# Moving value loads and reordering the first units in a fused attention and SwiGLU kernel

## The chip, the cores and the metric

The kernel runs on one core of a Trainium2 chip. The metric is the device time of one execution in microseconds. A profile, taken by the hardware profiler, covers the span from the first to the last instruction, which is a little shorter than the device time. The engines are TensorE (PE in the profile; its weight loads are PEld), VectorE (DVE), ScalarE (ACT), GpSimd (POOL) and SyncE (SP).

## The reference

The reference is attention with a sliding window and a few sink positions, followed by a SwiGLU feed-forward block. The batch is 4, there are 8 heads of 64, the sequence is 768, the window is 128 and there are 4 sinks.

```python
scores = scale * np.matmul(q, k.transpose(0, 1, 3, 2))
keep = is_sink | in_window          # pos < 4, or 0 <= row - pos < 128
scores = np.where(keep, scores, -1000000000.0)
scores = scores - np.max(scores, axis=-1, keepdims=True)
a = np.exp(scores)
a = a / (np.sum(a, axis=-1, keepdims=True) + 1e-09)
attn = np.matmul(a, v)
# x: 3072 tokens x 512, the heads side by side
g = x @ w_gate                      # 512 x 1536
silu = g * (1.0 / (1.0 + np.exp(-g)))
val = x @ w_val                     # 512 x 1536
out = silu * val @ w_out            # 1536 x 512
```

All inputs and the output are float32; the kernel computes its matrix products in bfloat16.

## The kernel before

The tokens are worked on in 12 groups of 256 (three for each batch entry). For a group, `step_T` or `step_TN` transposes keys and queries, `step_S` makes scores and exponentials, `step_PV` multiplies with the values and normalises, and `step_X` transposes the result for the projections. Group 0 has an opening of its own (`pair_T`, `pair_S`, `pair_mask`), which the change leaves alone. The projections are made in units: `gate` makes 512 columns of the gate projection (`gate_a`), takes the attention steps that the schedule hangs on that unit, and makes the value projection and the product (`gate_b`). Blocks 0 and 1 are the tokens of groups 0 and 1, at 256 tokens each; "01" means both together. A unit at f of block 0 covers f and f + 1, and each weight pair `load_gate(i)` holds two values of f, so that units f = 0, 2, 4 of a block need weight pairs 0, 1, 2.

[...] `later` is a list of VectorE work put off until `flush`. All loads on `nc.gpsimd` go out from GpSimd in program order and convert float32 to bfloat16 on the way. [...]

```python
    def load_rows(g):
        b, c = divmod(g, GC)
        x = new_rows(g)
        for i in range(2):
            for w in range(2):
                nc.gpsimd.dma_start(
                    x[64 * w:64 * (w + 1), i],
                    by_rows((k, q)[i], b, w, ALL, c * 256))


    ...

    def load_v(g):
        b, c = divmod(g, GC)
        va = vpool.tile([P, 2, H, VS], BF16, tag=f"va{g}", name="va")
        nc.vector.memset(va[:, :, :, D:D + 1], 1.0)
        for j in range(2):
            t0 = c * 256 + j * P
            nc.gpsimd.dma_start(
                va[:, j, :, 0:D], v[b, :, t0:t0 + P].rearrange("h p d -> p h d"))
        vas[g] = va

    ...

    load_sinks(vcf, 0, 1)
    for i in range(2):
        nc.gpsimd.dma_start(x0[:, i, 4:8], by_two((k, q)[i], 4))
    nc.gpsimd.iota(tq, [[1, P]], base=0, channel_multiplier=0,
                   allow_small_or_imprecise_dtypes=True)
    nc.gpsimd.iota(tk, [[0, 1]], base=0, channel_multiplier=1,
                   allow_small_or_imprecise_dtypes=True)
    load_rows(1)
    load_v(0)
    nc.gpsimd.iota(th8, [[-32, 4], [-NS, 4]], base=0, channel_multiplier=1,
                   allow_small_or_imprecise_dtypes=True)
    load_gate(0)
    load_gate(1, (0,))
    load_v(1)
    load_gate(1, (1,))
    load_gate(2)
    nc.gpsimd.tensor_copy(out=vcf[64:128], in_=vcf[0:64])

    ...

    def step_T(g, i, p2, evict=None):
        b, c = divmod(g, GC)
        new_T(b)
        x = rows[g]
        pt = bank([P, 2, 256], FP32, "pt")
        for pp in range(2):
            p = 2 * p2 + pp
            for r in range(4):
                for w in range(2):
                    h = slice(64 * w, 64 * (w + 1))
                    nc.tensor.matmul(
                        pt[h, pp, r:256:4], x[h, i, p, r * D:(r + 1) * D],
                        ident[h, h], start=True, stop=True, skip_group_check=True)
        dst = (kTs, qTs)[i][b][:, 2 * p2:2 * p2 + 2, c * 256:(c + 1) * 256]
        if (evict or ("a", "v")[i]) == "a":
            nc.scalar.copy(out=dst, in_=pt)
        else:
            nc.vector.tensor_copy(out=dst, in_=pt)

    ...

    def step_S(g, p2):          # scores of four heads, exp on ScalarE, mask on VectorE later
        ...
        pss = [bank([P, 512], FP32, "s") for _ in range(4)]
        for pp in range(2):
            p = 2 * p2 + pp
            for kk, qq, n, col in parts:
                for h in range(2):
                    r = slice(h * D, (h + 1) * D)
                    nc.tensor.matmul(
                        pss[2 * pp + h][:, col:col + n], kTs[b][r, p, kk:kk + P],
                        qTs[b][r, p, qq:qq + n], start=True, stop=True)
        ...
        for pp in range(2):
            h0 = 4 * p2 + 2 * pp
            for h in range(2):
                nc.scalar.activation(
                    e_t[g][:, h0 + h, lo:512], pss[2 * pp + h][:, lo:512],
                    AF.Exp, scale=scale)

            def dve(e=e_t[g][:, h0:h0 + 2, lo:512]):
                nc.vector.tensor_tensor(
                    e, e, m[:, :, lo:512].broadcast_to([P, 2, 512 - lo]), op=ALU.mult)
            later.append(dve)


    ...

    def step_PV(g, j, hh, norm="v"):   # P@V of four heads of one 128-row half
        ...
        xn = xns[g, j][:, 256 * hh:256 * (hh + 1)].rearrange("p (h d) -> p h d", h=4)

        def dve():
            rcp = smallp.tile([P, 4, 1], FP32, tag="rcp", name="rcp")
            nc.vector.reciprocal(rcp, po[:, :, D:D + 1])
            if norm == "a":
                for hq in range(4):
                    nc.scalar.activation(
                        xn[:, hq], po[:, hq, 0:D], AF.Copy, scale=rcp[:, hq])
            else:
                nc.vector.tensor_tensor(
                    xn, po[:, :, 0:D], rcp.broadcast_to([P, 4, D]), op=ALU.mult)
        if norm == "a":
            dve()
        else:
            later.append(dve)


    ...

    def project(ws, tb, f, name):
        n = xTs[tb].shape[2]
        ps = bank([P, 512], FP32, name)
        for i in range(512 // n):
            fi, fo = FOF[f + i]
            for c in range(DMC):
                nc.tensor.matmul(
                    ps[:, i * n:(i + 1) * n], ws[fi][:, c, fo * P:(fo + 1) * P],
                    xTs[tb][:, c], start=(c == 0), stop=(c == DMC - 1))
        return ps

    def gate_a(tb, f):
        if tb not in hts:
            n = SIZES[tb]
            t = hpool.tile([P, DFC * 512], BF16, tag="ht", name="ht")
            hts[tb] = dense(t, DFC, n)
            if tb == 0:
                hts["01"] = t.rearrange("p (b c n) -> p b c n", b=2, c=DFC)
                hts[1] = t[:, DFC * n:2 * DFC * n].rearrange("p (c n) -> p c n", c=DFC)
        pg = project(wgs, tb, f, "pg")
        th = tpool.tile([P, 512], FP32, tag="th", name="th")
        nc.scalar.activation(th, pg, AF.Tanh, scale=0.5)
        return pg, th

    def gate_b(tb, f, pg, th):
        pv = project(wvs, tb, f, "pv")
        u = upool.tile([P, 512], BF16, tag="u", name="u")
        nc.vector.scalar_tensor_tensor(u, th, 1.0, pg, op0=ALU.add, op1=ALU.mult)
        if tb == "01":
            nc.vector.tensor_tensor(
                hts[tb][:, :, f], *(x.rearrange("p (b n) -> p b n", b=2) for x in (u, pv)),
                op=ALU.mult)
            return
        nc.vector.tensor_tensor(
            hts[tb][:, f:f + 512 // SIZES[tb]].rearrange("p a n -> p (a n)"), u, pv,
            op=ALU.mult)

    def gate(tb, f, attn):
        a = gate_a(tb, f)
        for step in attn:
            step()
        gate_b(tb, f, *a)
        flush()

    def both(one_, two_, attn):

        a = [gate_a(*x) for x in (one_, two_)]
        for x, y in zip((one_, two_), a):
            gate_b(*x, *y)
        flush()

    ...

    def pro(*steps):
        for s in steps:
            s()
            if len(later) > 1:
                later.pop(0)()

    ...

    pair_S(3, 2)
    for p in range(1, NP2):
        pair_mask(p)
    nc.vector.tensor_scalar(lt8, th8, float(NS), None, op0=ALU.is_lt)
    nc.vector.scalar_tensor_tensor(lt8, th8, 0.0, lt8, op0=ALU.is_ge, op1=ALU.mult)
    nc.vector.tensor_reduce(diag_h, lt8.rearrange("p q h -> p h q"), mybir.AxisListType.X,
                            op=ALU.max)
    step_vsb(0)
    load_nat(2)
    load_gate(3)
    load_v(2)
    load_gate(4)
    load_gate(5)
    for i in range(4):
        load_out(i)
    step_T(1, 0, 0, "a")
    step_T(1, 0, 1, "a")
    step_T(1, 1, 0, "a")
    step_PV(0, 0, 0)
    step_PV(0, 0, 1)
    flush()
    step_T(1, 1, 1, "a")
    step_ks(0)
    step_PV(0, 1, 0)
    step_PV(0, 1, 1)
    flush()
    step_S(1, 0)
    masks1 = list(later)
    later.clear()
    step_X(0, 0)
    step_X(0, 1)
    flush()
    step_S(1, 1)
    later[:0] = masks1
    flush()
    load_nat(3)
    load_v(3)
    nc.gpsimd.memset(vcl, 0.0)
    nc.gpsimd.memset(vcl[:, :, D:D + 1], 1.0)
    load_sinks(vcl, 1, B)

    g0, g1, g2 = gates(0), gates(1), gates(2)
    us = [g0[0], g0[1], (alone, 0, 0), (both, g0[2][1:], g1[0][1:]), g1[1],
          g1[2], *((gate, "01", f) for f in range(6, DFC)),
          *g2, *downs(0), *downs(1), *downs(2)]

    ...

    weave(us, slots(
        (0, [K(1)]), (1, [A(step_PV, 1, 0, 0), A(step_PV, 1, 0, 1, "a"), A(step_PV, 1, 1, 0),
                              A(step_PV, 1, 1, 1, "a"), flush]),
        (2, [A(step_X, 1, 0, "a"), A(step_X, 1, 1, "now")]),
        ((4, 4, 5, 5), TN(2)), ((6, 7), Ss(2)), (6, [K(2)]),
        ...
```

The whole kernel follows.

Of the kernel before, what the change touches and what calls it, by code (L numbers as in the profile page):

```python
# [14 lines left out]
def kernel(  # L15
# [12 lines left out]
    nc = tc.nc  # L28
# [66 lines left out]
    def load_rows(g):  # L95
        b, c = divmod(g, GC)
        x = new_rows(g)
        for i in range(2):
            for w in range(2):
                nc.gpsimd.dma_start(  # L100
                    x[64 * w:64 * (w + 1), i],
                    by_rows((k, q)[i], b, w, ALL, c * 256))
# [90 lines left out]
    load_rows(1)  # L193
    load_v(0)
    nc.gpsimd.iota(th8, [[-32, 4], [-NS, 4]], base=0, channel_multiplier=1,
                   allow_small_or_imprecise_dtypes=True)
    load_gate(0)
    load_gate(1, (0,))
    load_v(1)
    load_gate(1, (1,))  # L200
# [9 lines left out]
    def flush():  # L210
        for f in later:
            f()
        later.clear()
# [208 lines left out]
    def gate_a(tb, f):  # L422
        if tb not in hts:
            n = SIZES[tb]
            t = hpool.tile([P, DFC * 512], BF16, tag="ht", name="ht")
            hts[tb] = dense(t, DFC, n)
            if tb == 0:
                hts["01"] = t.rearrange("p (b c n) -> p b c n", b=2, c=DFC)
                hts[1] = t[:, DFC * n:2 * DFC * n].rearrange("p (c n) -> p c n", c=DFC)
        pg = project(wgs, tb, f, "pg")  # L430
        th = tpool.tile([P, 512], FP32, tag="th", name="th")
        nc.scalar.activation(th, pg, AF.Tanh, scale=0.5)  # L432
        return pg, th

    def gate_b(tb, f, pg, th):
        pv = project(wvs, tb, f, "pv")
# [18 lines left out]
    def both(one_, two_, attn):  # L455

        a = [gate_a(*x) for x in (one_, two_)]
        for x, y in zip((one_, two_), a):
            gate_b(*x, *y)
        flush()  # L460
# [139 lines left out]
    for p in range(1, NP2):  # L600
        pair_mask(p)
    nc.vector.tensor_scalar(lt8, th8, float(NS), None, op0=ALU.is_lt)
# [9 lines left out]
    for i in range(4):  # L612
        load_out(i)
    step_T(1, 0, 0, "a")
    step_T(1, 0, 1, "a")
    step_T(1, 1, 0, "a")
    step_PV(0, 0, 0)
    step_PV(0, 0, 1)
    flush()
    step_T(1, 1, 1, "a")  # L620
    step_ks(0)
    step_PV(0, 1, 0)
    step_PV(0, 1, 1)
    flush()
    step_S(1, 0)
    masks1 = list(later)
    later.clear()
    step_X(0, 0)
    step_X(0, 1)
    flush()  # L630
    step_S(1, 1)
    later[:0] = masks1
    flush()
# [7 lines left out]
    us = [g0[0], g0[1], (alone, 0, 0), (both, g0[2][1:], g1[0][1:]), g1[1],  # L641
          g1[2], *((gate, "01", f) for f in range(6, DFC)),
# [8 lines left out]
    def NV(g):  # L651
# [3 lines left out]
        (0, [K(1)]), (1, [A(step_PV, 1, 0, 0), A(step_PV, 1, 0, 1, "a"), A(step_PV, 1, 1, 0),  # L655
                              A(step_PV, 1, 1, 1, "a"), flush]),
        (2, [A(step_X, 1, 0, "a"), A(step_X, 1, 1, "now")]),
        ((4, 4, 5, 5), TN(2)), ((6, 7), Ss(2)), (6, [K(2)]),
        ((8, 8), PVs(2)[:2]), (9, [A(step_PV, 2, 0, 1, "a"), A(step_PV, 2, 1, 1, "a")]),
        ((10, 11), [A(step_X, 2, 0, "a"), A(step_X, 2, 1, "a")]),  # L660
        (11, [NV(4), lambda: nc.gpsimd.tensor_copy(out=vcl[64:128], in_=vcl[0:64])]), ((14, 14, 15, 15), TN(3, "aa")),
        (15, [A(xbar, 4)]), (15, [NV(5)]), (19, [A(xbar, 5)]), (19, [NV(6)]),
        (23, [A(xbar, 6)]), (23, [NV(7)]),
        ((17, 18), Ss(3)), (18, [A(step_ks, 1)]), (18, [A(step_vsb, 1)]),
        ((19, 19, 19, 20), PVs(3)), (20, Xs(3)),
        ((19, 20), Ss(4)), (19, [K(4)]),
        ((21, 21, 22, 22), PVs(4)), (22, Xs(4))))
# [56 lines left out]
```

## Time and profile before

| what | value |
|---|---|
| median of 3 runs | 238.88 us (238.76 to 239.7) |
| span of the profiled execution | 237.3 us |
| mean granted TensorE clock | 0.998 |
| PE idle, span from 0 to 30 us | 2.79 us (27.21 busy of 30.00) |
| moved over the span | 27.36 MB, mean 115 GB/s |

The page gives for each engine its busy time and share of the span, and digits for 40 equal slices of the span, of about 5.9 us each. The change touches the first five or six slices. Four rows of digits show the opening against the rest (tenths of busy time for the engines; for DMA the mean busy share of the 16 DMA engines):

```profile
DVE  4888778768652888960798980688970598877000
ACT  4896485467452836512845622655622663333221
POOL 8996865720807107080260700080000000000000
DMA  8999999994999999999499994599204100200132
```

In the groups of the page, "u<-th,pg" is the first of two VectorE products of a unit (tanh plus one, times the gate projection), "ht<-u,pv" the second. "e<-s" is the exponential of scores, "e<-e,mask" the mask, "xn<-o,rcp" the normalisation of P@V, "px" and "xT" the transposed result. A timeline row gives start, duration, engine, line, operation, tiles and count, and in brackets the idle time before it with what ended it.

### The profile page before, as it was taken

The page shows a single profiled execution, that of the slowest core. Times are in us where ns is not written, and L with a number is a line of the kernel's source. Part 1 is how long each engine was busy: PE and PEld are TensorE (multiplying, and loading weights), DVE is VectorE, ACT ScalarE, POOL GpSimd, SP SyncE. Part 2 cuts the span into 40 slices and gives each one's busy share as a digit, 9 for nine tenths or more (in the row PEclk, how much of TensorE's full clock was granted, in tenths as well). Part 3 has the DMA queues.
Part 4 walks back from the last instruction along what each step waited for, and adds up shares of the span by engine and source line. Part 5 has one row for each costly group of instructions (what it writes and reads, how often), then busy time and mean ns, then how long its engine had stood idle before and what let it go on. Part 6 is the DMA issues. An engine that isn't in the chain of part 4 may idle for free.

```text
span 237.3 us, 4886 instructions
## 1 busy us (share of the span) xinstructions
PE 229.4 (97%) x1874; PEld 127.3 (54%) x1901; DVE 157.9 (67%) x335; ACT 114.5 (48%) x237; POOL 74.5 (31%) x98
## 2 busy tenths in 40 slices
PE   7899999999999999999999999999999999999994
PEld 4577845795554444444444444444444445488443
DVE  4888778768652888960798980688970598877000
ACT  4896485467452836512845622655622663333221
POOL 8996865720807107080260700080000000000000
PEclk9999999999999999999999999999999999999999
DMA  8999999994999999999499994599204100200132
GB/s 140 152 179 178 180 200 205 159 148 74 132 138 202 155 130 107 138 118 239 112 123 114 116 73 145 138 96 137 40 21 139 64 3 0 44 3 1 52 127 89
DMA packets 107655, 27.36 MB, mean 115 GB/s; under 512 B 94704, under 2 KB 104688, under 8 KB 107632
## 3 DMA queue, kind: packets, MB, share of 16 engines
q0 software_dynamic: 76640, 13.90, 79.0%
q1 hardware_dynamic: 30448, 12.89, 27.6%
q8 instruction: 15, 0.25, 0.4%
q10 hardware_dynamic: 544, 0.26, 0.4%
q14 instruction: 8, 0.07, 0.1%
HBM read 28.34 MB, written 6.29 MB: 146 GB/s over the span
## 4 chain that ended last, share of the span: by engine, by line
PE 88%; ACT 5%; DVE 2%; issue 1%; DMA 1%; SPq 0%; DVEq 0%; ACTq 0%
PE pd L475 26%; PE pv L417 26%; PE pg L417 25%; PE o L355 4%; PE s L292 4%; ACT e L299 2%; DMA st<-in_k_dram 1%; ACT e L572 1%; PE pn L245 1%; ACT xn L366 1%; PE o L335 1%; PE pk L320 1%; ACT th L432 1%; DVE u L438 1%; PE px L396 0%
## 5 line engine op out<-in xcount | busy, mean ns | idle before, releaser
L438 DVE SCALAR_TENSOR_TENSOR u<-th,pg 128x512 bf16<-128x512 f32 x72 | 49.1, 682 | 39.2 <-ACT th L432 39.2
L417 PE MATMUL pv<-xT,wv 128*128 128x512 bf16 (+1 forms) x351 | 73.0, 336 | 0.9 <-DMA wv<-in_moe_w_val_dram 0.4
L417 PE MATMUL pg<-xT,wg 128*128 128x512 bf16 (+1 forms) x351 | 73.1, 335 | 0.7
L432 ACT ACTIVATE th<-pg 128x512 f32<-128x512 f32 x72 | 43.5, 604 | 62.4 <-PE pg L417 58.7
L475 PE MATMUL pd<-wo,ht 128*128 128x512 bf16 (+2 forms) x291 | 64.8, 370 | 0.4
L444 DVE TENSOR_TENSOR ht<-u,pv 128x512 bf16<-128x512 bf16 x66 | 45.4, 688 | 10.4 <-PE pv L417 3.5
L417 PEld LDWEIGHTS <-wg 128*128 128x128 bf16 x360 | 35.0, 98 | 28.2 <-issue 0.9
L299 ACT ACTIVATE e<-s 128x512 bf16<-128x512 f32 (+1 forms) x88 | 42.7, 583 | 3.5 <-PE s L292 3.5
L475 PEld LDWEIGHTS <-ht 128*128 128x128 bf16 x300 | 27.9, 98 | 29.9 <-issue 0.5
L417 PEld LDWEIGHTS <-wv 128*128 128x128 bf16 x360 | 32.0, 98 | 21.1 <-issue 1.7
L111 POOL DMA_DIRECT2D nat<-in_k_dram x20 | 17.6, 887 | 75.9 <-DMA qT<-nat 72.9
L480 ACT ACTIVATE ot<-pd 128x512 f32<-128x512 f32 (+1 forms) x24 | 14.3, 596 | 47.4 <-PE pd L475 43.4
L304 DVE TENSOR_TENSOR e<-e,mask 128x1024 bf16<-128x1024 bf16 (+1 forms) x44 | 27.2, 651 | 4.2 <-ACT e L299 4.2
L122 POOL DMA_DIRECT2D va<-in_v_dram x24 | 21.5, 920 | 4.3 <-DMA wo<-in_moe_w_out_dram 2.5
L369 DVE TENSOR_TENSOR xn<-o,rcp 128x256 bf16<-128x256 f32 x44 | 18.7, 424 | 1.5
L355 PEld LDWEIGHTS <-e 128*128 128x128 bf16 x352 | 15.0, 98 | 7.8 <-DVE va L119 0.2
L111 POOL DMA_DIRECT2D nat<-in_q_dram x20 | 17.7, 896 | 1.4 <-DMA wg<-in_moe_w_gate_dram 0.8
L355 PE MATMUL o<-va,e 128*128 128x65 bf16 x352 | 17.0, 193 | 0.2
L292 PE MATMUL s<-qT,kT 64*128 64x128 bf16 (+1 forms) x240 | 12.9, 237 | 0.0
L292 PEld LDWEIGHTS <-kT 64*128 64x128 bf16 x240 | 7.7, 94 | 7.6 <-issue 6.6
L482 DVE TENSOR_SCALAR ot<-pd 128x128 f32<-128x128 f32 x1 | 0.3, 291 | 14.3 <-PE pd L475 14.3
L363 DVE RECIPROCAL rcp<-o 128x4 f32<-128x4 f32 x48 | 8.1, 174 | 1.7 <-PE o L355 1.6
(73 smaller groups left out, 92.1 us busy)
## 6 DMA issues: line engine op xcount, KB each, us to landing
out_dram<-ot SPq DMA_DIRECT2D x23, 256.0 KB
va<-in_v_dram POOLq DMA_DIRECT2D x24, 128.0 KB, 6.3
nat<-in_k_dram POOLq DMA_DIRECT2D x20, 128.0 KB, 4.6
nat<-in_q_dram POOLq DMA_DIRECT2D x20, 128.0 KB, 5.5
wg<-in_moe_w_gate_dram POOLq DMA_DIRECT2D x6, 256.0 KB, 8.0
wv<-in_moe_w_val_dram POOLq DMA_DIRECT2D x6, 256.0 KB, 8.5
wo<-in_moe_w_out_dram POOLq DMA_DIRECT2D x4, 384.0 KB, 11.8
st<-in_q_dram ACTq DMA_DIRECT2D x2, 128.0 KB
```

The lines of the kernel that those rows point to most:

```text
L111: nc.gpsimd.dma_start(x[:, i, j].rearrange("p (h d) -> p h d", d=D), src[b, :, t0:t0 + P].rearrange("h p d -> p h d"))
L122: nc.gpsimd.dma_start(va[:, j, :, 0:D], v[b, :, t0:t0 + P].rearrange("h p d -> p h d"))
L292: nc.tensor.matmul(pss[2 * pp + h][:, col:col + n], kTs[b][r, p, kk:kk + P], qTs[b][r, p, qq:qq + n], start=True, stop=True)
L299: nc.scalar.activation(e_t[g][:, h0 + h, lo:512], pss[2 * pp + h][:, lo:512], AF.Exp, scale=scale)
L304: nc.vector.tensor_tensor(e, e, m[:, :, lo:512].broadcast_to([P, 2, 512 - lo]), op=ALU.mult)
L355: nc.tensor.matmul(o, l, r, start=(c == 0 and i == 0), stop=(i == len(mms) - 1), skip_group_check=True)
L369: nc.vector.tensor_tensor(xn, po[:, :, 0:D], rcp.broadcast_to([P, 4, D]), op=ALU.mult)
L417: nc.tensor.matmul(ps[:, i * n:(i + 1) * n], ws[fi][:, c, fo * P:(fo + 1) * P], xTs[tb][:, c], start=(c == 0), stop=(c == DMC - 1))
L432: nc.scalar.activation(th, pg, AF.Tanh, scale=0.5)
L438: nc.vector.scalar_tensor_tensor(u, th, 1.0, pg, op0=ALU.add, op1=ALU.mult)
L444: nc.vector.tensor_tensor(hts[tb][:, f:f + 512 // SIZES[tb]].rearrange("p a n -> p (a n)"), u, pv, op=ALU.mult)
L475: nc.tensor.matmul(po, hts[tb][:, f, ts * P:(ts + 1) * P], wos[f // n][:, f % n, lo:hi], start=(f == 0), stop=(f == DFC - 1))
```

## The change

The order of loads changes in the opening: the values of group 0 are issued between the keys and the queries of group 1, and the values of group 1 ahead of both halves of the second weight pair. The attention steps follow: P@V and transpose of group 0 come before the transposes of group 1's queries, one normalisation of group 0 moves to ScalarE, and the VectorE work that makes `diag_h` moves behind them. The second half of group 1's scores moves into the first projection unit. That unit makes its gate and value projections but holds back its two VectorE products (`gate_held`) until group 1 is transposed, so that these products do not stand before group 1's masks and reciprocals on VectorE. The units that need the second weight pair come after group 1's P@V. The unit `both` is dropped, and every later unit has an index higher by one in the schedule, with the same steps. The purpose is to have TensorE work on what has been loaded while it would otherwise wait.

```diff
--- before.py
+++ after.py
@@ -92,14 +92,14 @@
         rows[g] = rowp.tile([P, 2, NP2, 4 * D], BF16, tag="rows", name="rows")
         return rows[g]
 
-    def load_rows(g):
-        b, c = divmod(g, GC)
-        x = new_rows(g)
-        for i in range(2):
-            for w in range(2):
-                nc.gpsimd.dma_start(
-                    x[64 * w:64 * (w + 1), i],
-                    by_rows((k, q)[i], b, w, ALL, c * 256))
+    def load_rows(g, i):
+        b, c = divmod(g, GC)
+        if g not in rows:
+            new_rows(g)
+        for w in range(2):
+            nc.gpsimd.dma_start(
+                rows[g][64 * w:64 * (w + 1), i],
+                by_rows((k, q)[i], b, w, ALL, c * 256))
 
     def load_nat(g):
         b, c = divmod(g, GC)
@@ -190,14 +190,14 @@
                    allow_small_or_imprecise_dtypes=True)
     nc.gpsimd.iota(tk, [[0, 1]], base=0, channel_multiplier=1,
                    allow_small_or_imprecise_dtypes=True)
-    load_rows(1)
+    load_rows(1, 0)
     load_v(0)
+    load_rows(1, 1)
     nc.gpsimd.iota(th8, [[-32, 4], [-NS, 4]], base=0, channel_multiplier=1,
                    allow_small_or_imprecise_dtypes=True)
     load_gate(0)
-    load_gate(1, (0,))
     load_v(1)
-    load_gate(1, (1,))
+    load_gate(1)
     load_gate(2)
     nc.gpsimd.tensor_copy(out=vcf[64:128], in_=vcf[0:64])
 
@@ -420,6 +420,10 @@
         return ps
 
     def gate_a(tb, f):
+        new_h(tb)
+        return tanh(project(wgs, tb, f, "pg"))
+
+    def new_h(tb):
         if tb not in hts:
             n = SIZES[tb]
             t = hpool.tile([P, DFC * 512], BF16, tag="ht", name="ht")
@@ -427,13 +431,16 @@
             if tb == 0:
                 hts["01"] = t.rearrange("p (b c n) -> p b c n", b=2, c=DFC)
                 hts[1] = t[:, DFC * n:2 * DFC * n].rearrange("p (c n) -> p c n", c=DFC)
-        pg = project(wgs, tb, f, "pg")
+
+    def tanh(pg):
         th = tpool.tile([P, 512], FP32, tag="th", name="th")
         nc.scalar.activation(th, pg, AF.Tanh, scale=0.5)
         return pg, th
 
     def gate_b(tb, f, pg, th):
-        pv = project(wvs, tb, f, "pv")
+        gate_v(tb, f, pg, th, project(wvs, tb, f, "pv"))
+
+    def gate_v(tb, f, pg, th, pv):
         u = upool.tile([P, 512], BF16, tag="u", name="u")
         nc.vector.scalar_tensor_tensor(u, th, 1.0, pg, op0=ALU.add, op1=ALU.mult)
         if tb == "01":
@@ -452,12 +459,15 @@
         gate_b(tb, f, *a)
         flush()
 
-    def both(one_, two_, attn):
-
-        a = [gate_a(*x) for x in (one_, two_)]
-        for x, y in zip((one_, two_), a):
-            gate_b(*x, *y)
-        flush()
+    held = []
+
+    def gate_held(tb, f, attn):
+
+        new_h(tb)
+        pg = project(wgs, tb, f, "pg")
+        for step in attn:
+            step()
+        held.append(A(gate_v, tb, f, *tanh(pg), project(wvs, tb, f, "pv")))
 
     def down(tb, ts, attn, last=False):
         at = {}
@@ -599,6 +609,21 @@
     pair_S(3, 2)
     for p in range(1, NP2):
         pair_mask(p)
+    step_T(1, 0, 0, "a")
+    step_T(1, 0, 1, "a")
+    step_ks(0)
+    step_PV(0, 0, 0)
+    flush()
+    step_PV(0, 0, 1, "a")
+    step_PV(0, 1, 0)
+    step_PV(0, 1, 1)
+    flush()
+    step_X(0, 0)
+    flush()
+    step_T(1, 1, 0, "a")
+    step_T(1, 1, 1, "a")
+    step_X(0, 1)
+    flush()
     nc.vector.tensor_scalar(lt8, th8, float(NS), None, op0=ALU.is_lt)
     nc.vector.scalar_tensor_tensor(lt8, th8, 0.0, lt8, op0=ALU.is_ge, op1=ALU.mult)
     nc.vector.tensor_reduce(diag_h, lt8.rearrange("p q h -> p h q"), mybir.AxisListType.X,
@@ -611,26 +636,7 @@
     load_gate(5)
     for i in range(4):
         load_out(i)
-    step_T(1, 0, 0, "a")
-    step_T(1, 0, 1, "a")
-    step_T(1, 1, 0, "a")
-    step_PV(0, 0, 0)
-    step_PV(0, 0, 1)
-    flush()
-    step_T(1, 1, 1, "a")
-    step_ks(0)
-    step_PV(0, 1, 0)
-    step_PV(0, 1, 1)
-    flush()
     step_S(1, 0)
-    masks1 = list(later)
-    later.clear()
-    step_X(0, 0)
-    step_X(0, 1)
-    flush()
-    step_S(1, 1)
-    later[:0] = masks1
-    flush()
     load_nat(3)
     load_v(3)
     nc.gpsimd.memset(vcl, 0.0)
@@ -638,8 +644,8 @@
     load_sinks(vcl, 1, B)
 
     g0, g1, g2 = gates(0), gates(1), gates(2)
-    us = [g0[0], g0[1], (alone, 0, 0), (both, g0[2][1:], g1[0][1:]), g1[1],
-          g1[2], *((gate, "01", f) for f in range(6, DFC)),
+    us = [(gate_held, *g0[0][1:]), (alone, 0, 0), g0[1], g1[0], g1[1], g0[2], g1[2],
+          *((gate, "01", f) for f in range(6, DFC)),
           *g2, *downs(0), *downs(1), *downs(2)]
 
     def L(*fs):
@@ -652,19 +658,21 @@
         return L(A(load_nat, g), A(load_v, g))
 
     weave(us, slots(
-        (0, [K(1)]), (1, [A(step_PV, 1, 0, 0), A(step_PV, 1, 0, 1, "a"), A(step_PV, 1, 1, 0),
-                              A(step_PV, 1, 1, 1, "a"), flush]),
-        (2, [A(step_X, 1, 0, "a"), A(step_X, 1, 1, "now")]),
-        ((4, 4, 5, 5), TN(2)), ((6, 7), Ss(2)), (6, [K(2)]),
-        ((8, 8), PVs(2)[:2]), (9, [A(step_PV, 2, 0, 1, "a"), A(step_PV, 2, 1, 1, "a")]),
-        ((10, 11), [A(step_X, 2, 0, "a"), A(step_X, 2, 1, "a")]),
-        (11, [NV(4), lambda: nc.gpsimd.tensor_copy(out=vcl[64:128], in_=vcl[0:64])]), ((14, 14, 15, 15), TN(3, "aa")),
-        (15, [A(xbar, 4)]), (15, [NV(5)]), (19, [A(xbar, 5)]), (19, [NV(6)]),
-        (23, [A(xbar, 6)]), (23, [NV(7)]),
-        ((17, 18), Ss(3)), (18, [A(step_ks, 1)]), (18, [A(step_vsb, 1)]),
-        ((19, 19, 19, 20), PVs(3)), (20, Xs(3)),
-        ((19, 20), Ss(4)), (19, [K(4)]),
-        ((21, 21, 22, 22), PVs(4)), (22, Xs(4))))
+        (0, [K(1), A(step_S, 1, 1), flush]),
+        (1, [A(step_PV, 1, 0, 0), A(step_PV, 1, 1, 0), A(step_PV, 1, 0, 1, "a"),
+             A(step_PV, 1, 1, 1, "a")]),
+        (2, [A(step_X, 1, 0, "a"), A(step_X, 1, 1, "now"), lambda: held.pop()()]),
+        (5, TN(2)[::2]), (6, TN(2)[1::2]), ((7, 8), Ss(2)), (7, [K(2)]),
+        ((9, 9), PVs(2)[:2]), (10, [A(step_PV, 2, 0, 1, "a"), A(step_PV, 2, 1, 1, "a")]),
+        ((11, 12), [A(step_X, 2, 0, "a"), A(step_X, 2, 1, "a")]),
+        (12, [NV(4), lambda: nc.gpsimd.tensor_copy(out=vcl[64:128], in_=vcl[0:64])]),
+        ((15, 15, 16, 16), TN(3, "aa")),
+        (16, [A(xbar, 4)]), (16, [NV(5)]), (20, [A(xbar, 5)]), (20, [NV(6)]),
+        (24, [A(xbar, 6)]), (24, [NV(7)]),
+        ((18, 19), Ss(3)), (19, [A(step_ks, 1)]), (19, [A(step_vsb, 1)]),
+        ((20, 20, 20, 21), PVs(3)), (21, Xs(3)),
+        ((20, 21), Ss(4)), (20, [K(4)]),
+        ((22, 22, 23, 23), PVs(4)), (23, Xs(4))))
 
     def pair(ga, gb, sh=0):
         s = sh
```

## Prediction

> **What bounds the kernel now.** I read the page first, then the chain of waits and the engine timelines of the opening, then the landing times of single transfers.
>
> The page, busy time by engine:
>
> ```profile
> PE 229.4 (97%) x1874; PEld 127.3 (54%) x1901; DVE 157.9 (67%) x335; ACT 114.5 (48%) x237; POOL 74.5 (31%) x98
> ...
> PEclk9999999999999999999999999999999999999999
> ```
>
> TensorE is busy nearly all the time at full clock, so a change of order can win only the time in which TensorE stands still, and loses every microsecond that it adds to that. The change ends where the two orders meet again, at the matmuls of f 6 (29.5 us of the span); what happens there is shifted, and TensorE is then continuously fed. So the question is when TensorE gets there. The chain of waits from 8 to 24 us says what sets the opening:
>
> ```profile
> 11.35 0.40 PE o L355 x8
> 11.75 0.56 PE pt L230 x16
> 12.31 0.59 PE o L355 x16
> 12.91 0.37 PE s L292 x6
> 13.28 4.03 ACT e L299 x8
> 17.31 0.03 issue
> 17.33 0.69 DVE e L304
> 18.02 0.62 DVE u L438
> ...
> 19.55 1.75 ACT xn L366 x8
> 21.30 0.05 issue
> 21.35 0.23 PE px L396
> 21.58 0.87 PE pg L417 x8
> ```
>
> Not TensorE but ScalarE carries it: eight exponentials of group 1 (4.03/8 = 0.504 us each), the mask, then eight ScalarE normalisations (0.22 each), before group 1 can be transposed and its tokens projected. TensorE beside it (start, duration, instruction, count, wait):
>
> ```profile
> 8.74 1.32 PE L230 MATMUL pt<-ident,rows 64*64 64x64 bf16 x33
> 10.63 0.63 PE L230 MATMUL pt<-ident,rows 64*64 64x64 bf16 x15 [0.57 <-DMA rows<-in_q_dram]
> ...
> 18.24 1.15 PE L355 MATMUL o<-va,e 128*128 128x65 bf16 x32
> 19.76 1.05 PE L417 MATMUL pv<-xT,wv 128*128 128x256 bf16 x8 [0.38 <-DMA wv<-in_moe_w_val_dram]
> ```
>
> Between 8.74 and 23.34 (14.6 us) it has 12.4 us of work, by the durations in this timeline: 64 row transposes 2.56, P@V of group 0 0.95 and of group 1 1.15 plus sinks 0.24, four output transposes 0.92, scores 1.1, K 0.24, six projections at 0.87 = 5.2. So 2.2 us at most could be won. The two named waits are 0.57 (group 1's queries) and 0.38 (second value weights).
>
> Last, when transfers land. The second query half of group 1 and the first half of group 0's values:
>
> ```profile
> L100 POOL DMA_DIRECT2D rows<-in_q_dram x2: 655/661/667, 4.5 to 5.1; - x2
> ...
> DMA to landing us min/median/max: 5.2/5.4/5.5
> ```
>
> ```profile
> L122 POOL DMA_DIRECT2D va<-in_v_dram x1: 973/973/973, 5.7 to 5.7; - x1
> ...
> DMA to landing us min/median/max: 5.5/5.5/5.5
> ```
>
> The queries are complete at 5.1 + 5.5 = 10.6, where TensorE resumes; the two value halves at 11.2 and 6.6 + 5.5 = 12.1. I read the other transfers in the same way: keys 8.2 and 9.0, first weights 13.6 and 15.4, second gate weights 16.8, group 1's values 17.6 and 18.5, second value weights 19.7, third pair 21.1 and 22.7. One lands every 0.8 us (128 KB) or 1.3 to 1.8 us (256 KB), and time to landing grows to 9.7 us: a queue with a backlog, in the order of issue.
>
> [...] a moved transfer changes places in the queue, and what is let past it is paid by the others. [...] the reciprocals of group 1 start at 19.34, after the product of unit 0 (18.73 + 0.69), though the first of group 1's P@V blocks was done near 18.6. [...] the largest gap here is 0.6 and I expect none above 1.6[...]. [...] here the 97% hides the 2.2 us just counted.
>
> **The change part by part.** No matmul is added or removed. One normalisation of group 0 (four ScalarE instructions, 4 x 0.22 = 0.88) replaces one of VectorE (0.42).
>
> *Loads.* Values of group 0 take the queries' places: they land near 9.7 and 10.6 in place of 11.2 and 12.1, and the queries near 11.3 and 12.1 in place of 9.7 and 10.6. The queries lose 1.5 us. Group 1's values pass the second gate weights: values near 16.2 and 17.1, gate weights near 18.4.
>
> *Group 0, and group 1's queries.* TensorE: key transposes to 10.05 as before; P@V of group 0 (first block on masks and values, 24 matmuls, last two blocks on the second half at 10.6) to about 11.3. The block normalised by ScalarE: key copies end at 10.79, two sink-key copies to 11.2, normalisation to 12.1. So the first output transpose starts at 12.2, and the query transposes behind it: 12.45 to 13.7 (32 x 0.04); TensorE idles 0.9. The second output transpose ends at 13.95, scores of the first half 14.5. ScalarE: query copies end at 13.7 and 14.3, so exponentials start at 14.35 in place of 13.28: +1.07.
>
> *Exponentials.* The sinks' exponential (0.38) now comes between the two halves, while the first tanh moves behind them: 8 x 0.504 + 0.35 from 14.35 ends at 18.75, in place of 17.31. Last mask 19.45. TensorE in that time has only first gate projection 0.9, K 0.25, second scores 0.55, value projection 0.87, sinks 0.25 and two P@V blocks 0.6, 3.4 us from 14.5 to 19.45: about 1.4 us idle. Two half blocks are left, to 19.95.
>
> *Group 1's normalisation and transposes.* What the held unit is for: u and its product (0.62 + 0.69 with issue, 1.4 us) no longer stand before the reciprocals on VectorE. But the reciprocal and product of the first block do (0.55 from 19.5), so ScalarE's eight instructions run from about 20.25 to 22.0 (before 19.55 to 21.30): the 1.4 us late has become 0.7. Transposes of group 1 end near 22.3 (before 21.58), with one projection (0.87) done in the P@V gap. Then value projection 0.87 to 23.2; ScalarE does the tanh of unit 2 (0.6) and the copy of the transpose (0.64), to 23.25; group 1's first gate projection starts near 23.3.
>
> *Sum.* Before, that projection starts at 22.45, and the gate projection of g0[2] (0.87) has been done; after, at 23.3 without it. Lag 0.85 + 0.87 = 1.7 us. The idle time gives the same: about 0.2 + 0.9 + 1.4 + 0.35 + 0.6 + 0.1 = 3.6 against 2.2, so 1.4. The floor: if ScalarE never waited from the end of the first query transposes (13.1) on, it would have copies 1.2, exponentials 4.4, two tanh 1.2, normalisations 1.75, copy 0.64 = 9.2, ending at 22.3; lag 0.7. I take the middle, a little down for small waits later (0.15 at 35.3, others of 0.05) that can take up some of a lag: +1.1 us.
>
> **The rivals.** (a) *The order wins.* It takes both named waits away (0.57 + 0.38), and diag_h's three VectorE instructions (0.8 from 10.41) from before group 0's P@V. If the exponentials started no later than now, the freed VectorE would bring ScalarE's normalisations forward and a gain of 0.5 to 1 us would come out: 238.0 to 238.4. For it: VectorE is in the chain twice for u and product. Against it: the queries are the first link of ScalarE's 4 us, and they give way to values that nothing in ScalarE's chain awaits. (b) *Even:* queries land 0.5 us sooner than I think, or va1's earlier landing and the 0.88 us projection fill the gap: 238.6 to 239.2. For it: the DMA digits of the page are at 9 in nearly every slice of the opening, so the moved transfers only change places and later needs are unchanged. (c) *Worse:* banks. Unit 0's gate and value results stay in two of eight PSUM banks until unit 2; the four P@V banks may have to wait for exponentials of the second half (second one near 17.8). I expect that to hide in the 1.4 us gap; if not, the lag is 2 us or more: 241. (d) *diag_h later* (near 15.2 in place of 11.2), so the sink-value product on GpSimd ends near 15.8 and group 2's loads are issued about 0.9 later; time to landing is over 8 us then, so a backlog hides it.
>
> **Range and chances.** 238.88 + 1.1 = 240.0. For the range: floor lag 0.7 less 1.1 for a wrong landing estimate gives 238.5; full lag 1.7 plus 0.5 for banks gives 241.1. Two per cent is 4.8 us; the whole idle time of the opening is 2.2, so a gain of that size is impossible, and a loss of it would need a further wait of 3 us. Faster 0.01, within 0.97, slower 0.02. Of the direction I am about three quarters sure.
>
> **What would show it.** Queries complete near 12.1 and TensorE waiting for them or the normalisation for about 0.9 us; first exponential of group 1 near 14.3 and last ending near 18.75; a TensorE gap of over 1 us before the second half of group 1's P@V, released by the mask or ScalarE; group 1's transposes near 22.1; first group 1 projection near 23.3; f 6 reached 1 to 1.7 us later than 29.5. I am wrong if the queries land before 11.5, if the exponentials start before 13.8, or if f 6 starts before 29.5; and on the size if TensorE's later gaps swallow the lag.

## The result, and the profile after

| | before | after |
|---|---|---|
| median | 238.99 us (6 runs, 238.76 to 239.7) | 240.2 us (6 runs, 239.72 to 240.52) |
| ratio | | 1.0045, 95% interval 1.0028 to 1.0061 |
| profiled span | 237.3 us | 238.4 us |
| first exponential of group 1 starts | 13.27 | 14.35 |
| last exponential of group 1 ends | 17.30 | 18.55 |
| f 6 starts on TensorE | 29.47 | 30.58 |

The changed kernel is slower by 0.45 per cent, 1.2 us. TensorE's busy time is nearly the same (page after; columns as before):

```profile
PE 229.9 (96%) x1874; PEld 128.2 (54%) x1901; DVE 157.5 (66%) x334; ACT 115.3 (48%) x241; POOL 74.5 (31%) x98
...
PEclk9999999999999999999999999999999999999999
```

The time is lost before f 6: the lag there is 1.11 us, the lag of the whole span 1.1 us. How much of it is standing time is read from the stretch up to f 6 and the part of it up to group 1's key transposes, before, after, and in a second profile of the changed kernel (each row: stretch, length, busy us of PE, PEld, DVE, ACT and POOL with the number of instructions, granted clock, DMA share, GB/s):

```profile
0.00:29.47 29.47, 26.74 (x349) 19.92 (x350) 22.66 (x64) 19.44 (x46) 24.91 (x39) 1.00 1.57 166
0.00:8.74 8.74, 7.37 (x66) 4.14 (x66) 5.50 (x22) 5.08 (x12) 7.64 (x17) 1.00 0.94 143
...
0.00:30.58 30.58, 27.37 (x350) 20.82 (x351) 21.93 (x63) 20.18 (x50) 26.02 (x41) 1.00 1.59 168
0.00:9.09 9.09, 7.83 (x67) 4.98 (x67) 5.34 (x22) 5.14 (x12) 7.99 (x18) 1.00 1.19 143
...
0.00:30.32 30.32, 26.88 (x349) 20.30 (x350) 21.97 (x63) 20.20 (x50) 25.67 (x40) 1.00 1.58 169
0.00:8.83 8.83, 7.36 (x66) 4.46 (x67) 5.39 (x22) 5.14 (x12) 7.73 (x17) 1.00 1.14 145
```

TensorE stood idle for 2.73 us before and 3.21 after. The other 0.63 us is longer busy time, and 0.46 of that lies ahead of the key transposes (7.83 against 7.37), where group 0's opening is unchanged. In the second profile that part is gone (7.36), idle time is 3.44, and so 0.71 of its lag of 0.85 is standing time. From the key transposes to f 6 both profiles of the changed kernel take 21.49 us; the first merely started 0.26 later. So about a quarter of the 1.11 comes and goes between executions of one and the same kernel.

The chain of waits of the opening after (start, us, what):

```profile
11.43 0.94 ACT xn L366 x4
12.37 0.05 issue
12.41 0.23 PE px L396
12.64 1.01 PE pt L230 x32
13.66 0.33 PE px L396 x4
13.99 0.37 PE s L292 x6
14.36 2.05 ACT e L299 x4
16.41 0.17 ACT es L324
16.58 1.97 ACT e L299 x4
...
18.57 0.69 DVE e L304
...
19.94 1.75 ACT xn L366 x8
21.70 0.05 issue
21.74 0.23 PE px L396
21.97 0.87 PE pv L417 x8
22.85 0.89 PE pg L417 x8
```

It is the same chain as before, exponentials, mask, normalisation, transposes, but its head has changed: the query transposes (pt) now follow a ScalarE normalisation of group 0 and an output transpose. ScalarE's last exponential ends 1.25 us later. On TensorE the gap is there (timeline after):

```profile
17.22 0.66 PE L335 MATMUL o<-vsb,es 32*128 32x260 bf16 x4
17.81 0.83 PE L355 MATMUL o<-va,e 128*128 128x65 bf16 x20
19.32 0.54 PE L355 MATMUL o<-va,e 128*128 128x65 bf16 x12 [0.68 <-DVE e L304]
```

The last twelve P@V matmuls wait 0.68 us for the last mask. When the second half of group 1's queries landed (issue rows after, start and time to landing): 6.9 + 4.9 = 11.8.

```profile
L100 POOL DMA_DIRECT2D rows<-in_q_dram x1: 685/685/685, 6.9 to 6.9; - x1
...
DMA to landing us min/median/max: 4.9/4.9/4.9
```

TensorE takes the queries only at 12.6. The gap between landing and use is a matter of order, not of the queue; an experiment below removes it.

### The profile page after: what moved, and what is told of

Same layout as the page of the kernel before. It is cut to its first block, busy times and chain, and to the rows that moved or that the text cites. A ratio compares the mean times of both kernels' runs of the same rounds, so it can differ in the third digit from the quotient of the medians.

```text
span 238.4 us, 4887 instructions
## 1 busy us (share of the span) xinstructions
PE 229.9 (96%) x1874; PEld 128.2 (54%) x1901; DVE 157.5 (66%) x334; ACT 115.3 (48%) x241; POOL 74.5 (31%) x98
## 4 chain that ended last, share of the span: by engine, by line
PE 90%; ACT 5%; DVE 2%; issue 1%; DVEq 0%; ACTq 0%
PE pd L485 26%; PE pv L417 26%; PE pg L417 25%; PE s L292 4%; PE o L355 4%; ACT e L299 2%; PE w L545 1%; ACT xn L366 1%; PE pt L561 1%; PE pn L245 1%; ACT e L582 1%; PE o L335 1%; PE px L396 1%; PE pk L320 1%; ACT th L437 1%
## 5 line engine op out<-in xcount | busy, mean ns | idle before, releaser
L490 ACT ACTIVATE ot<-pd 128x512 f32<-128x512 f32 (+1 forms) x24 | 14.3, 596 | 47.4 <-PE pd L485 43.4
L369 DVE TENSOR_TENSOR xn<-o,rcp 128x256 bf16<-128x256 f32 x43 | 18.3, 425 | 1.5
L492 DVE TENSOR_SCALAR ot<-pd 128x128 f32<-128x128 f32 x1 | 0.3, 291 | 14.3 <-PE pd L485 14.3
```

The lines of the kernel that those rows point to most:

```text
L369: nc.vector.tensor_tensor(xn, po[:, :, 0:D], rcp.broadcast_to([P, 4, D]), op=ALU.mult)
```

## The experiments

Theory Q: the late start of group 1's exponentials is the cost. Theory U: the new order of units and weights is. Each ratio is against the kernel before, run beside it on the same chip; "f 6" is its start in the profile. The last two columns are from one profile each: with the loads and the opening up to the first scores as before (the kernel before itself, second half in its second profile, units only, hold only, packed, transposes first) the exponentials start anywhere from 12.73 to 13.27, so a few tenths of a microsecond there decide nothing.

| run | median us | before us | ratio (95%) | exponentials of group 1 | f 6 |
|---|---|---|---|---|---|
| loads only | 240.3 | 239.13 | 1.0050 (1.0032 to 1.0069) | 15.30 to 19.3 | 31.7 |
| first half | 240.13 | 239.13 | 1.0041 (1.0025 to 1.0057) | 14.64 to 18.7 | 30.83 |
| second half | 239.99 | 239.13 | 1.0041 (1.0019 to 1.0064) | see second profile | |
| second half, second profile | 239.88 | 239.38 | one run | 13.09 to 18.32 | 30.34 |
| units only | 239.36 | 239.38 | 0.9997 (0.9978 to 1.0017) | 13.10 to 17.1 | 29.44 |
| queries first | 239.69 | 239.13 | 1.0035 (1.0017 to 1.0053) | 13.78 to 18.0 | 30.02 |
| gap filled | 239.72 | 239.38 | 1.0008 (0.9990 to 1.0026) | 14.50 to 18.7 | 30.80 |
| gap filled, copy first | 240.06 | 239.28 | 1.0026 (1.0005 to 1.0047) | 14.04 to 18.2 | 29.61 |
| hold only | 240.19 | 239.38 | 1.0030 (1.0014 to 1.0046) | 12.97 to 17.0 | 30.46 |
| packed | 239.5 | 239.28 | 1.0009 (0.9989 to 1.0028) | 12.73 to 16.8 | 29.81 |
| packed, transposes first | 239.28 | 239.38 | 0.9997 (0.9984 to 1.0009) | 12.80 to 16.8 | 28.53 |
| changed kernel again | 240.05 | 239.28 | 1.0029 (1.0014 to 1.0044) | 14.09 to 18.3 | 30.32 |

### Loads only

```diff
 # the kernel before
-    load_rows(1)
+    load_rows(1, 0)
     load_v(0)
+    load_rows(1, 1)
```

> The kernel before with one edit: group 0's values are issued between group 1's keys and queries; every engine's order is that of before. Theory Q (the queries' place in the DMA queue sets the start of group 1's exponentials, and ScalarE's chain from there sets when TensorE reaches f 6): the queries are complete at 11.8 in place of 10.6, TensorE stands still from about 10.1 to 11.8, the first exponential of group 1 starts near 14.3 in place of 13.3, f 6 starts near 30.5 in place of 29.5, and the time is 240.0 (239.7 to 240.4). Theory U (the new order of the units and the moved second weight pair cost the time): 239.0, as before.

The place in the queue alone costs 0.50 per cent, as much as the whole change. Q held, U's number fell. The profiled run shows one thing that Q did not foresee. Stretches of 1 us in and after TensorE's waits of 1.05 and 0.49 us for the queries (columns as above):

```profile
11.00:12.00 1.00, 0.32 (x5) 0.18 (x7) 0.29 (x3) 0.11 (x1) 1.00 (x2) 1.00 1.32 168
12.00:13.00 1.00, 1.00 (x30) 0.85 (x31) 0.18 (x1) 0.41 (x1) 1.00 (x2) 1.00 1.41 194
13.00:14.00 1.00, 1.00 (x23) 0.83 (x20) 0.93 (x4) 0.41 (x2) 0.96 (x3) 0.53 1.35 175
14.00:15.00 1.00, 1.00 (x20) 0.85 (x19) 0.66 (x4) 0.66 (x3) 0.92 (x3) 0.50 1.52 185
15.00:16.00 1.00, 1.00 (x14) 0.70 (x11) 0.48 (x2) 0.70 (x2) 1.00 (x2) 0.50 2.13 164
16.00:17.00 1.00, 1.00 (x19) 0.77 (x16) 0.73 (x2) 1.00 (x3) 1.00 (x2) 0.77 2.23 165
```

The granted clock fell to 0.50 for over 3 us after waits of 1.54 us in all, and the exponentials began at 15.30 rather than near 14.3. Three of eight runs had a mean clock of 0.993 and took 240.8 to 241.4 us. The other five took 239.7 to 240.4, and their median, 240.13, is 0.42 per cent above the kernel before; so that much stands without the clock. There is no profile of this run at full clock.

### First half

```diff
 # the kernel before, loads as above; diag_h, its product and the loads behind it
+    step_T(1, 0, 0, "a")   step_T(1, 0, 1, "a")   step_ks(0)
+    step_PV(0, 0, 0); flush()
+    step_PV(0, 0, 1, "a"); step_PV(0, 1, 0); step_PV(0, 1, 1); flush()
+    step_X(0, 0); flush()
+    step_T(1, 1, 0, "a")   step_T(1, 1, 1, "a")
+    step_X(0, 1); flush()
+    # diag_h ... load_out
+    step_S(1, 0)   step_S(1, 1)   flush()
 # ... and the same steps leave their old places
```

> The first half of the change alone: values of group 0 before the queries, and P@V and first output transpose of group 0 before the query transposes, diag_h behind them; the units, the second weight pair and the second half of the scores are as before. Q: the exponentials start near 14.3 and the time is 240.1 (239.7 to 240.5); what TensorE does while it waits buys nothing, since ScalarE's chain is what is late. U: 239.0 to 239.3.

240.13, as Q said. My reading of the traces is that the work of group 0 which TensorE now does while it waits had room later, beside ScalarE's exponentials: ahead of the P@V of group 1 TensorE now stands still for 0.98 us, until ScalarE has made the sinks' exponential, where it did not wait before.

### Second half, and a second profile of it

```diff
 # the changed kernel
-    load_rows(1, 0); load_v(0); load_rows(1, 1)
+    load_rows(1, 0); load_rows(1, 1); load_v(0)
 # opening as before up to step_S(1, 0) and both step_X; step_S(1, 1) stays in unit 0
```

> The second half of the change alone: the queries in their old place, the opening's TensorE order of before up to the first half of group 1's scores, then the units of the change with the held products, group 1's values ahead of the second weight pair, the second scores within unit 0. Q: the exponentials start near 13.3 as before, and the time is that of before within 0.4 (238.6 to 239.4). U: 240.0 to 240.4.

Q's number fell: with the queries in their old place the second half alone still costs 0.41 per cent. In its first profile a transfer of values landed late (TensorE waited 1.21 us for it) and the granted clock fell to 0.50 for about 7 us (0.986 on the mean of that execution), which hides the cause. Two theories for the cost: P, the second scores stand too late on TensorE; O, the order of the units and of the weights costs the time. A second profile:

> The second half alone once more, for an undisturbed profile (in the first one a transfer of group 0's values landed 1.2 us late). P: the first exponential starts near 13.3, a gap of ScalarE of about 1 us lies between the fourth exponential and the fifth, which waits for the scores, and the last ends near 18.5. O: no such gap, and TensorE waits for the second weight pair instead.

ScalarE's timeline in the second profile:

```profile
13.09 2.06 ACT L299 ACTIVATE e<-s 128x512 bf16<-128x512 f32 x4
15.94 0.28 ACT L324 ACTIVATE es<-pk 128x128 bf16<-128x128 f32 x1 [0.78 <-PE pk L320]
16.25 2.07 ACT L299 ACTIVATE e<-s 128x512 bf16<-128x512 f32 x4
```

The first half of the exponentials starts as early as before, and then ScalarE stands still for 0.78 us: the scores of the second half come behind unit 0's gate projection, which itself waited 0.52 us for group 0's transposed output, and behind K. The end of the exponentials, 18.32, is almost that of the changed kernel. This is what theory P expects; it is tested next.

### Units only

```diff
 # the second half
+    step_S(1, 1)
+    later[:0] = masks1
+    flush()
-        (0, [K(1), A(step_S, 1, 1), flush]),
+        (0, [K(1)]),
```

> The second half of the change alone, but with the second half of group 1's scores back in the opening, right behind group 0's output transposes. Theory P (what cost the second half its time is that the second scores stand behind unit 0's gate projection and K on TensorE, which wait for group 0's transposed output, so that ScalarE stands still between the two halves of its exponentials): the eight exponentials run without a gap from about 13.3 to 17.4 and the time is 239.1 (238.7 to 239.4). Theory O (the order of the units and of the second weight pair costs the time): 239.8 to 240.2, as in the second half alone.

0.9997, and the exponentials are whole again, eight in 4.03 us from 13.10. P held: of the second half it is the place of the second scores that costs. The order of the units, the held products and the exchange of values and second gate weights together cost nothing that can be measured, and bring nothing; the interval leaves 0.2 per cent either way. In the profile the normalisations do start earlier (18.80, before 19.55) and group 1's first projection too (21.56, before 22.45), but with four projections done by then in place of five, and one is 0.87 us. That also says why the two halves do not add up: late queries and late second scores delay the same last four exponentials, and with the queries late the second scores are ready in time (in the changed kernel, es at 16.41 and the next exponential at 16.58 follow without a gap).

### Queries first

```diff
 # the changed kernel
-    step_X(0, 0)
-    flush()
     step_T(1, 1, 0, "a")
     step_T(1, 1, 1, "a")
+    step_X(0, 0)
+    flush()
```

> The changed kernel with one edit: group 1's query transposes stand ahead of group 0's first output transpose on TensorE. Theory N (in the changed kernel TensorE's program order holds the queries back behind ScalarE's normalisation of group 0 and its transpose, to 12.6, though they land near 11.8): query transposes start near 11.8, exponentials near 13.6, f 6 near 29.9, time 239.5 (239.2 to 239.8). Theory L (the landing alone sets it): within 0.25 of the changed kernel, 240.0 to 240.4.

The timeline of TensorE in it:

```profile
11.65 1.22 PE L230 MATMUL pt<-ident,rows 64*64 64x64 bf16 x32
12.80 0.62 PE L396 MATMUL px<-ident,xn 128*128 128x128 bf16 x8
13.35 0.62 PE L292 MATMUL s<-qT,kT 64*128 64x128 bf16 x12
```

The queries are taken at 11.65, the exponentials start at 13.78, f 6 at 30.02: 0.56 earlier than in the first profile of the changed kernel and 0.30 than in its second. In time it is 0.35 per cent above the kernel before, where the changed kernel had 0.45 and 0.29. N is shown in the profile; in the times the gain is within the intervals.

### Hold only

```diff
 # the kernel before
-    us = [g0[0], g0[1], ...
+    us = [(gate_held, *g0[0][1:]), g0[1], ...
-                              A(step_PV, 1, 1, 1, "a"), flush]),
+                              A(step_PV, 1, 1, 1, "a"), flush, lambda: held.pop()()]),
```

> The kernel before with one idea of the change alone: unit 0's two VectorE products are put behind group 1's reciprocals and normalisations. Theory H: group 1's ScalarE normalisations start near 19.0 in place of 19.55, the wait of 0.15 before the last transpose of group 1 goes, but the value projection waits for its weights to 19.7 all the same; 238.95 (238.7 to 239.2). Rival: the products stand in the way for 1.4 us and taking them away brings 0.5 us or more, 238.6 or less.

Both theories missed: 0.30 per cent slower. The normalisations do start early, at 18.82. But the two held products, and those of the next unit behind them, now stand on VectorE before the copy of group 1's second transpose (VectorE's timeline):

```profile
20.26 0.68 DVE L446 SCALAR_TENSOR_TENSOR u<-th,pg 128x512 bf16<-128x512 f32 x1
20.98 0.69 DVE L452 TENSOR_TENSOR ht<-u,pv 128x512 bf16<-128x512 bf16 x1
21.58 0.68 DVE L446 SCALAR_TENSOR_TENSOR u<-th,pg 128x512 bf16<-128x512 f32 x1
22.36 0.69 DVE L452 TENSOR_TENSOR ht<-u,pv 128x512 bf16<-128x512 bf16 x1
22.97 0.42 DVE L404 COPY xT<-px 128x512 bf16<-128x512 bf16 x1
```

and TensorE waits for that copy:

```profile
23.44 1.05 PE L418 MATMUL pg<-xT,wg 128*128 128x256 bf16 x8 [1.41 <-DVE xT L404]
```

Work that is put off is not gone. In the changed kernel the held products (from 22.35) come behind this copy (22.01), and TensorE doesn't wait for it.

### Gap filled, and the copy first

```diff
 # queries first; unit 1 becomes
+        p0(); p1()                 # P@V of heads 0 to 3, both row halves
+        a = gate_a(0, 2)           # in the gap before the last masks
+        p2(); p3(); flush()
+        held.pop()()
+        pv = project(wvs, 0, 2, "pv")
+        x0(); c = gate_a(0, 4); x1()
+        # products of g0[2 to 3], then gate (1, 0), values and products of (0, 4) and (1, 0)
```

> The changed kernel with the query transposes first, and with the gate projection of g0[2 to 3] put between the two halves of group 1's P@V, the held products right behind group 1's reciprocals, and the gate projection of g0[4] between the two transposes of group 1. If the lag is TensorE standing still behind ScalarE while projections whose weights have landed wait behind it in its order, these two projections (0.87 each, about 1.1 of it into gaps of 0.7 and 0.6) bring the time to 238.7 (238.3 to 239.1). If instead the late start of ScalarE's chain can't be filled because the weights (landing near 18.1 and 20.9) or PSUM banks hold the projections back, 239.4 to 239.8, as with the queries first alone.

Even with the kernel before (1.0008), but above the first range expected; 239.72 lies in the second, in which weights or banks hold the projections back. In its profile, which is of the slowest of the fourteen runs (240.43), the queries landed at 12.4, and the second gate weights, issued at 10.93 with 8.2 to landing, at 19.1: the projection meant for the gap started at 19.23. The timeline of the matmuls puts that wait down to ScalarE's tanh, which ended at 19.19, but the weight loads of this projection are shown waiting for the transfer:

```profile
19.22 0.77 PEld L417 LDWEIGHTS <-wg 128*128 128x128 bf16 x8 [0.72 <-DMA wg<-in_moe_w_gate_dram]
```

So the weights held the projection back in this profile, whether or not the tanh would have done so as well. The 0.52 us wait for VectorE's copy is there too. Putting tanh and held products behind the copies:

> The gap-filled form of the changed kernel (queries early on TensorE, but late in the queue) with the copies of the transposed halves ahead of the held products and the tanhs. If VectorE's held products ahead of the copy cost the 0.5 us wait seen in the gap-filled profile, the time goes from even with the kernel before to 0.3 to 0.6 below it; if the queries' late landing (11.8) bounds all of it, it stays even within 0.2.

1.0026, a miss. The 0.52 us wait was still there, since on TensorE itself the second transpose stood behind the gate projection of g0[4], with nothing to cover its copy. That the timed median (240.06) lies above the profiled run (239.14) isn't explained.

### Packed, and the transposes first

```diff
 # units only; unit 1 becomes
+        pro(p0, p1, p2, p3); flush()
+        pg, pv = project(wgs, 0, 2, "pg"), project(wvs, 0, 2, "pv")
+        x0()
+        pc = project(wgs, 0, 4, "pg")      # transposes first: this line behind x1()
+        x1()
+        a = tanh(pg); held.pop()(); gate_v(0, 2, *a, pv)
+        c = tanh(pc); d = gate_a(1, 0); gate_b(0, 4, *c); gate_b(1, 0, *d)
```

> Queries in their old place, second scores in the opening, held products (as in the units alone), and the projections packed around group 1's transposes: gate and value projection of g0[2 to 3] directly behind group 1's P@V, the gate projection of g0[4] between the two transposes, the transposed halves copied ahead of the tanhs and of the held products. Theory G (with the exponentials starting at 13.3, what is left is TensorE's program order around the transposes): the waits of 0.4 and 0.2 before the transposes go, group 1's first projection starts near 21.7 with five projections done in place of four, and the time is 0.5 to 0.9 below the kernel before. Rival: the weights' landing (19.3, 20.6) and VectorE's debt of held products take the place of those waits; within 0.3 of the kernel before.

1.0009: the rival. The weights held the value projection up by 0.29 us, and TensorE waited 0.52 us for the copy. The other place of one line:

> The packed form with one exchange: both transposes of group 1 directly behind the value projection, and the gate projection of g0[4] behind them, so that it covers the copies of the transposed halves on ScalarE and VectorE. In the packed profile TensorE waited 0.52 us for the second copy before group 1's first projection. If TensorE's order around the transposes is all that is left, that wait goes and the time is 0.3 to 0.7 below the packed form, so 0.1 to 0.5 below the kernel before. If the weights' landing (near 19.6 and 20.9) bounds it, the wait turns up before the gate projection of g0[4] and the time stays within 0.15 of the kernel before.

In the profile the edit does what it should (TensorE's timeline): two gate projections follow the transposes without a wait, and f 6 starts at 28.53, 0.94 us before the kernel before.

```profile
20.14 0.61 PE L396 MATMUL px<-ident,xn 128*128 128x128 bf16 x8
20.64 1.92 PE L417 MATMUL pg<-xT,wg 128*128 128x256 bf16 x16
...
28.53 1.03 PE L417 MATMUL pg<-xT,wg 128*128 128x512 bf16 x4
```

Later it gives some back, to a transposing transfer of attention output that has not landed:

```profile
111.12 1.02 PE L417 MATMUL pg<-xT,wg 128*128 128x512 bf16 x4 [0.34 <-DMA xT<-xn]
```

The time is that of the second expectation, but its reason, a wait for weights ahead of the gate projection, isn't in the profile. The K matmuls of the group at 113.16 in the kernel before come at 112.62 here: a lead of 0.94 at 76 us has become 0.54. The profiled run, 238.58, was the lowest of 14; the median, 239.28, is even with the kernel before (0.9997). No version tried beats the kernel before by more than its interval. What takes the lead away in the timed runs was not seen and stays open.

### The changed kernel again

> The changed kernel itself beside them, on the same chip: 0.4 to 0.5 per cent above the kernel before, and in its profile the exponentials of group 1 from about 14.0 to 18.6 whether or not TensorE starts at half rate in this run, if the queries' landing and ScalarE's normalisation of group 0 set them.

0.29 per cent above the kernel before, lower than expected, its interval overlapping that of the first measurement. Here TensorE started the key transposes at 8.83 (8.74 before, 9.09 in the first profile after), so this is the cleaner profile: f 6 at 30.32, a lag of 0.85. Against the first profile the key transposes, the exponentials (14.09) and f 6 all come 0.26 earlier. So the start of the execution shifts this chain as a whole, against the expectation; and the queries' landing does not set it, since they landed near 11.4 here and were taken only at 12.32.

## Why the prediction was right

Predicted 240.0, which is +1.1 us; measured 240.2, +1.2, and the second time 240.05, +0.77 against 239.28. The mechanism is right, a late start of ScalarE's chain because the queries are transposed late, but the closeness of the number is in part luck: the lag at f 6 was 1.11 in one profile and 0.85 in the other, and the size was a choice between two sums. By its steps:

- **The queue.** Landing in the order of issue, queries late: right (keys at 7.5 and 8.4, values of group 0 at 9.1 and 10.4, queries at 11.0 and 11.8). The term was 1.5 us late, to 12.1; they landed at 11.8, 1.2 late, and near 11.4 in the second profile (6.9 + 4.5). That is earlier than 11.5, which I had named as a sign of being wrong, and it changed nothing, for the reason of the next step. The loads alone show that in the old order on TensorE this place in the queue costs as much as the whole change.
- **Queries behind the normalisation of group 0.** Predicted start 12.45, measured 12.6 and 12.3. Queries first confirms that the order, and not the landing, set the last part of it.
- **The exponentials.** 14.35 to 18.75 predicted, 14.35 to 18.55 measured, and 14.09 to 18.28 in the second profile. The exact 14.35 owes something to the slow start of the first.
- **The gap before group 1's second P@V half.** About 1.4 us predicted. From 17.10 to 19.32 TensorE was busy 1.43 of 2.22 us, so 0.8 idle; the four sink matmuls took 0.66 in place of 0.29 beside that. So the gap of over 1 us that was to show did not come. Whether waits for one of the eight buffers of the kernel's pool `psum`, rival (c), are behind the longer sinks was not tested; the only wait that the profile names there is the one of 0.68 for the mask.
- **The idle time.** 3.6 us after against 2.2 before was a sum of durations. From the key transposes to f 6 the profile counts 1.37 us idle before (20.73 less 19.36 busy), and 1.95 and 1.96 in the two profiles after: both the level and the growth of 1.4 were too large.
- **First projection of group 1.** This is the other term that was mis-sized: 23.3 and a lag of 0.85 + 0.87 = 1.7 predicted; measured 22.70 against 22.45, with one projection fewer, 0.25 + 0.87 = 1.1 (22.45 and 0.87 in the second profile). I put tanh and copy at 1.24 us behind normalisations ending at 22.0; these ended at 21.68, and the copy 0.97 later, at 22.65. The middle that I took, +1.1, was a choice between floor (0.7) and sum (1.7); f 6 came 1.11 later, and 0.85 in the second profile, below the 1 to 1.7 that was to show it.
- **After f 6.** No later gap swallowed the lag: K of group 2 at 32.08 against 30.98, the same K step further on at 114.17 against 113.16. Rival (d), the later loads of group 2, cost nothing that shows: after f 6 TensorE has the same two named waits as before, 0.25 us for scores and 0.17 (before 0.18) for exponentials.
- **What the prediction did not see.** The second scores in unit 0 are a cost by themselves, 0.41 per cent, hidden in the changed kernel because the queries are late as well. Undoing the first half alone, as I would have advised, would have brought nothing. And rival (a)'s advantage, VectorE freed of the held products, is worth nothing measurable here (units only, 0.9997).

## What to carry to other kernels

Where one engine's queue of work sets a stage (here 4 us of exponentials), rank the loads by when that engine can begin, not by what the idle engine could do meanwhile: filling the idle engine with work that had room later brought nothing here (first half, 1.0041). Two delays of the same chain hide one another, so undoing one half of a change tells little until the other half has been run alone. Work that is put off must be followed to where it lands on its engine: with the held products in front of the next copy on VectorE, TensorE waited 1.41 us for that copy (hold only); with them behind it, not at all (changed kernel).

## What the runs showed of the hardware

- TensorE's granted clock fell to half in two profiles; that it stays at 1.00 throughout, as the sums of the prediction take it, was an estimate. After 1.05 + 0.49 us of waiting in the loads-only profile it was 0.50 from about 13.1 to 16.5 (by the means of 0.53 and 0.77 in the rows at its ends). In the first profile of the second half it fell after a wait of 1.21 us (0.85 on the mean from 13 to 14, 0.50 to 20, 0.74 from 20 to 21, so low from about 13.7 to 20.5). But in hold only a wait of 1.41 us left it at 1.00 (1.000 on the mean of that execution), so the length of the wait alone does not decide it. What else does no run shows.
- At the start, TensorE ran slowly while the profile shows a granted clock of 1.00: the 14 matmuls on zeros with which the kernel opens took 3.17 us, 226 ns each, and a projection's eight of the same shape (128x256) later take 0.87, 109 ns each. How long this lasts differs from run to run: the first 16 transposes of group 0 took 1.92 us in the first profile of the changed kernel and, 0.15 us of waiting included, 1.48 in that of before, and up to the key transposes TensorE was busy 7.83 us in the first profile of the changed kernel and 7.36 in its second. From the key transposes to f 6 the two profiles of the changed kernel differ by a shift of 0.26 us, a quarter of the effect studied, so a single pair of profiles isn't enough at this size.
